# One batch for an expert product, a top-8 from the gate rows, and two groups of transposes moved from TensorE to DMA

## The chip, the cores and the metric

The kernel runs on one core of one Trainium2 chip. The metric is device time in microseconds (us) of one execution. The kernel before took 249.81 us (median of 3 runs, 249.35 to 250.25). A run also lists the span that the profile sees (some 1.8 us less than the time) and the mean clock granted to TensorE. A run is called slow when it is more than 1.5% above the fastest of its own kernel; ratios use fast runs only.

Names: PE is TensorE (matmuls), PEld its weight loads, DVE VectorE, ACT ScalarE, POOL GpSimd, SP SyncE, which only issues transfers here. Clock 1.00 is full speed.

## The reference

Two branches over the same 2048 rows of 1024 numbers, mixed by a gate. Branch A is a complex state-space scan; branch B adds an expert's output to eight chosen rows only.

```python
g = sigmoid((x * gate_w).sum(-1))                       # one gate per row
a = 2*Re(C @ scan(Lam_bar, B_bar @ x)) + x*Dskip        # the bulk of the work
idx = argsort(-(x @ w_r))[:8]                           # eight chosen rows
xs = x[idx]
y = (silu(xs @ w_gate) * (xs @ w_up)) @ w_down          # 1024 -> 3584 -> 1024
b = x;  b[idx] += y * sigmoid(r[idx])
out = g*a + (1-g)*b                                     # bf16, 1 x 2048 x 1024
```

Branch A keeps TensorE busy for almost the whole time. The expert must be squeezed between its matmuls.

## The kernel before

The program is a list of large blocks (`s1`: input product, `s2`: output product, each 16 matmuls of 128x512), and everything else is attached to positions in that list: `at((8, 1.9), f)` emits `f` in block 8 after its second piece. The parts that matter:

```python
def sel_c():                                   # eight chosen rows, transposed by PE
    for dc in range(KD):
        nc.tensor.transpose(xselT_ps[:, dc, :], xsel[:, dc*P:(dc+1)*P], ident[:NSEL, :NSEL])
    nc.scalar.copy(out=xselT[:, :, 0:NSEL], in_=xselT_ps[:])

def silu_t():                                  # the product silu(g)*u, transposed by PE
    for c in range(NFB):                       # NFB = 7
        nc.tensor.transpose(aT_ps[:, c]..., M["gr", 1][:, c*P:(c+1)*P], ident[:])
    nc.scalar.copy(out=M["aT"][:, :, :, 0:NSEL], in_=aT_ps[:, :, :, 0:NSEL])

# expert weights stream through slots of 1 MB (w_gate/w_up slots, then 7 of w_down);
# load_w() fills a slot from SP's queue as soon as its buffer is free
pos = [...] + [(8, 1.9)] * 4 + [(9, 2.9)] * 3  # y: first 64 matmuls, later 48

def skip_x(*bs):                               # rows scaled by (1-g): stored from ACT's queue
    nc.scalar.activation(out=xt[:], in_=xt[:], func=ACT.Copy, scale=omgcol[:, b:b+1])
    nc.scalar.dma_start(out2d[b*P:(b+1)*P, :], xt[:])
def fin(b):                                    # g*a added onto them: accumulating store, POOL
    nc.gpsimd.dma_start(out2d[b*P:(b+1)*P, :], ots.pop(b)[:], accum_op=ALU.add)
```

## Time and profile before

| before | value |
|---|---|
| span of the profiled execution | 248.3 us |
| PE busy | 242.7 us, 98% |
| DVE busy | 227.0 us, 91% |
| PE waits | 2.3 us in all, every one before 12 us |
| matmuls of y | 64 at 207.1 us, 48 at 226.3 us |
| last matmul of the last tile starts its run | 238.1 us |

The row to trust is PE's. The lines themselves, and what follows from them, stand in the prediction.

### The profile page before, as it was taken

To read this page: it belongs to the slowest core of one execution; us is meant where nothing else is said; L and a number is where in the kernel's file an instruction comes from. 1 tells how busy PE (TensorE), PEld (TensorE's weight loads), DVE (VectorE), ACT (ScalarE), POOL (GpSimd) and SP (SyncE) were. 2 spreads that over 40 slices of the span, in tenths; PEclk is the share of its full clock that TensorE was granted. 3 is DMA by queue.
4 is the path that set the end of the run, shared out by engine and by line. 5 is a ranking of instruction groups with operands and counts; after the bars stand their busy time and mean duration, and the time that the engine had idled before them with its cause. 6 is when DMAs were issued, how large, how long until landed. Compare 5 with 4: busy or idle time off the path is not lost.

```text
span 248.3 us, 3608 instructions
## 1 busy us (share of the span) xinstructions
PE 242.7 (98%) x1414; PEld 115.6 (47%) x1414; DVE 227.0 (91%) x231; ACT 117.4 (47%) x203; POOL 33.6 (14%) x50
## 2 busy tenths in 40 slices
PE   7899999999999999999999999999999999999995
PEld 5664444444444444444444444444444445445453
DVE  0899999999999999999999999999999999995954
ACT  3599973333345322282354571235267445537421
POOL 4000000000100003151402050100100211011810
PEclk9999999999999999999999999999999999999999
DMA  7999999999760000077976989877599972993053
GB/s 170 214 201 213 223 228 202 261 220 255 225 220 0 3 0 0 7 187 210 340 212 225 343 252 300 279 240 291 156 313 317 374 157 59 308 309 45 3 118 96
DMA packets 64193, 48.25 MB, mean 194 GB/s; under 512 B 49568, under 2 KB 51232, under 8 KB 64176
## 3 DMA queue, kind: packets, MB, share of 16 engines
q1 hardware_dynamic: 59120, 37.23, 55.5%
q0 software_dynamic: 3424, 7.90, 14.8%
q10 hardware_dynamic: 1632, 2.89, 3.8%
q8 instruction: 11, 0.18, 0.3%
q14 instruction: 6, 0.05, 0.1%
HBM read 27.55 MB, written 8.40 MB: 145 GB/s over the span
## 4 chain that ended last, share of the span: by engine, by line
PE 84%; DVE 7%; DMA 4%; SPq 3%; issue 0%; ACT 0%; DVEq 0%
PE zps L771 42%; PE vps L266 32%; DMA X<-in_A_x_dram 4%; PE zps L787 3%; PE pgu L660 3%; SPq L80 2%; PE vps L282 1%; PE y L672 1%; DVE U L302 1%; DVE U L313 1%; DVE H L340 1%; DVE U L338 1%; DVE H L336 1%; PE zr L487 1%; DVE S2tab L252 1%; DVE Ctab L251 1%
## 5 line engine op out<-in xcount | busy, mean ns | idle before, releaser
L771 PE MATMUL zps<-CT,H 128*128 128x512 bf16 x480 | 105.5, 379 | 0.0
L266 PE MATMUL vps<-X,BT 128*128 128x512 bf16 x480 | 105.1, 379 | 0.0
L266 PEld LDWEIGHTS <-BT 128*128 128x128 bf16 x480 | 46.4, 98 | 56.6 <-PE pgu L660 0.7
L771 PEld LDWEIGHTS <-H 128*128 128x128 bf16 x480 | 46.2, 98 | 56.3 <-issue 1.5
L313 DVE TENSOR_TENSOR_SCAN U<-d,U 128x2048 bf16<-128x2048 f32 (+2 forms) x22 | 62.0, 2860 | 1.0 <-DVE U L304 0.5
L273 ACT CAST V<-vps 128x512 bf16<-128x512 f32 x60 | 32.2, 588 | 56.3 <-PE vps L266 56.3
L776 ACT ACTIVATE ot<-zps,gcol 128x512 bf16<-128x512 f32 x30 | 20.6, 687 | 54.1 <-PE zps L771 54.1
L797 POOL DMA_DIRECT2D out_dram<-ot x14 | 13.0, 931 | 34.4 <-ACT ot L776 24.0
L303 DVE TENSOR_TENSOR V<-V,nTi 128x4096 bf16<-128x4096 bf16 (+2 forms) x11 | 16.7, 1517 | 0.5
L304 DVE TENSOR_TENSOR U<-U,V 128x4096 bf16<-128x4096 bf16 (+2 forms) x11 | 16.7, 1516 | 0.4
L302 DVE TENSOR_TENSOR U<-V,T2tab 128x4096 bf16<-128x4096 bf16 (+2 forms) x11 | 16.6, 1509 | 0.4
L338 DVE TENSOR_TENSOR U<-U,S2tab 128x4096 bf16<-128x4096 bf16 x7 | 16.0, 2292 | 0.2
L340 DVE TENSOR_TENSOR H<-H,U 128x4096 bf16<-128x4096 bf16 x7 | 16.0, 2292 | 0.2
L336 DVE TENSOR_TENSOR H<-U,Ctab 128x4096 bf16<-128x4096 bf16 x7 | 16.0, 2283 | 0.0
L745 ACT CAST zps<-xd 128x512 f32<-128x512 bf16 (+1 forms) x25 | 14.2, 575 | 3.2 <-ACT xt L732 2.9
L709 POOL DMA_DIRECT2D xt<-in_A_x_dram x12 | 7.1, 592 | 62.7 <-DMA out_dram<-xt 31.5
L732 ACT ACTIVATE xt<-xt,omgcol 128x1024 bf16<-128x1024 bf16 x12 | 13.8, 1146 | 0.0
L371 DVE TENSOR_TENSOR_SCAN U<-D,U 128x1024 bf16<-128x1024 f32 x4 | 8.9, 2271 | 0.1
L282 PE MATMUL vps<-X,BT 128*128 128x256 bf16 x64 | 7.5, 273 | 0.9 <-DMA X<-in_A_x_dram 0.6
L727 DVE TENSOR_TENSOR xd<-xt,Dbc 128x1024 bf16<-128x1024 bf16 x12 | 7.7, 682 | 0.3 <-ACT V L273 0.3
L282 PEld LDWEIGHTS <-BT 128*128 128x128 bf16 x64 | 6.1, 98 | 2.4 <-issue 0.7
L660 PE MATMUL pgu<-wgu,xsel 128*32 128x448 bf16 x128 | 7.2, 354 | 0.0
(161 smaller groups left out, 152.7 us busy)
## 6 DMA issues: line engine op xcount, KB each, us to landing
wgu<-in_B_w_gate_dram SPq DMA_DIRECT2D x16, 448.0 KB, 6.5
wgu<-in_B_w_up_dram SPq DMA_DIRECT2D x16, 448.0 KB, 5.8
wd<-in_B_w_down_dram SPq DMA_DIRECT2D x12, 512.0 KB, 7.6
out_dram<-ot POOLq DMA_DIRECT2D x14, 256.0 KB, 5.8
xt<-in_A_x_dram POOLq DMA_DIRECT2D x12, 256.0 KB, 4.2
out_dram<-xt ACTq DMA_DIRECT2D x10, 256.0 KB, 5.3
xt<-in_A_x_dram SPq DMA_DIRECT2D x4, 256.0 KB, 3.5
out_dram<-xt POOLq DMA_DIRECT2D x4, 256.0 KB, 3.4
```

The lines of the kernel that those rows point to most:

```text
L266: nc.tensor.matmul(o, lhsT=BT[pl][:, dc, ct * P:(ct + 1) * P], rhs=X[m][:, dc, k0 * LC:k1 * LC], start=(dc == 0), stop=(dc == KD - 1))
L273: nc.scalar.copy(out=V[k][:, :, ct, :], in_=vp[m, ct][:, :, kk, :])
L282: nc.tensor.matmul(vps[:, pl, c, :], lhsT=BT[pl][:, dc, ct * P:(ct + 1) * P], rhs=X[0][:, dc, k * LC:(k + 1) * LC], start=(dc == 0), stop= ...
L302: nc.vector.tensor_tensor(out=u, in0=v, in1=T2tab[:, :, c0:c1, :], op=ALU.mult)
L303: nc.vector.tensor_tensor(out=v, in0=v, in1=bc(nTi, c0, c1), op=ALU.mult)
L304: nc.vector.tensor_tensor(out=u, in0=u, in1=V[k][:, ::-1, c0:c1, :], op=ALU.add)
L313: nc.vector.tensor_tensor_scan(out=fl, data0=d0[:, c0:c1, :].rearrange("p c t -> p (c t)"), data1=fl, initial=0.0, op0=ALU.mult, op1=ALU.add)
L336: nc.vector.tensor_tensor(out=h, in0=g, in1=bc(Ctab, c0, c1), op=ALU.mult)
L338: nc.vector.tensor_tensor(out=g, in0=g, in1=S2tab[:, :, c0:c1, :], op=ALU.mult)
L340: nc.vector.tensor_tensor(out=h, in0=h, in1=G[k][:, ::-1, c0:c1, :], op=ALU.add)
L771: nc.tensor.matmul(zps[:], lhsT=H[k][:, pl, ct, tl * P:(tl + 1) * P], rhs=CT[pl][:, ct, dsl], start=(fresh and ct == 0 and pl == 0), stop= ...
L776: nc.scalar.activation(out=ots[b][:, dsl], in_=zps[:], func=ACT.Copy, scale=gcol[:, b:b + 1])
```

## The change

The intent is to take small work off PE. The gate vectors are transposed in a hole at the start; the top-8 search reads the gate rows as they lie; the chosen rows and the expert's product are transposed by DMA; y is computed in one batch. For that all seven `w_down` slots must be in SBUF together, so four of them go into the dead buffer of B (`BT`), and they are all loaded without a break.

```diff
+    vb_ps = ...; two nc.tensor.transpose(...)          # now ahead of s1x(1, 0)
 def sel_a():
-    nc.tensor.transpose(rT_ps[:], rcb[:], ident[:])
+    rT = rowp.tile([P, 2 * LC], F32); nc.scalar.copy(out=rT[:], in_=M["zrb"][:])
 def sel_b():
-    for k in range(2): nc.tensor.matmul(fl_ps[:, k, :], lhsT=ones16[:], ...)
+    nc.tensor.matmul(fl_ps..., lhsT=ones8[:], rhs=mm..., start=True, stop=True)
 def sel_c():
-    for dc in range(KD): nc.tensor.transpose(...)
-    nc.scalar.copy(out=xselT[:, :, 0:NSEL], in_=xselT_ps[:])
+    nc.sync.dma_start_transpose(xselT[:], xsel[:])
 def silu_t():
-    (seven nc.tensor.transpose, one nc.scalar.copy)
+    nc.sync.dma_start_transpose(M["aT"][:]..., M["gr", 1][:])
-    at((8, 0.8), silu_t)
+    at((7, 0.97), silu_t)
-    pos = ... [(8, 1.9)] * 4 + [(9, 2.9)] * 3
+    pos = ... [(8, 3.9)] * 7
+        if n == 7:                                      # B is dead: room for 4 slots
+            for pl in range(2):
+                t = const.tile([P, 4, 2, D], BF16, name="wdb", tag=f"BT{pl}")
+                free_w.extend(((t, 0), (t, 1)))
 ...                                                    # cuts: zs_ps moved to (8, 3.88), scatter earlier, skip_d(4) behind dve_m(5)
```

## The prediction

> **What bounds the kernel now.** I read the page's first part, then TensorE's waits, then the chain that ended last in order of time. The busy line of the page:
>
> ```profile
> PE 242.7 (98%) x1414; PEld 115.6 (47%) x1414; DVE 227.0 (91%) x231; ACT 117.4 (47%) x203; POOL 33.6 (14%) x50
> ```
>
> TensorE (PE) is busy for 242.7 of 248.3 us; VectorE (DVE) with 91% is second. All that PE waited for, from the view of PE's waits:
>
> ```profile
> PE wps L149 <- DVE halfpi L129: 1.1, 1, 1.1
> PE vps L282 <- DMA X<-in_A_x_dram: 0.6, 1, 0.6
> PE va_ps L161 <- DMA vrow<-in_A_Lambda_im_dram: 0.4, 1, 0.4
> PE vps L282 <- DMA BT<-in_A_B_im_dram: 0.2, 1, 0.2
> ```
>
> All four lie before 12 us. From 11.93 us to 245.24 us the chain is PE without a hole, apart from a detour over DVE at 36 to 61 us during which PE's own timeline is solid (208 matmuls of line 266 from 15.65 on). So a microsecond of PE work removed after 12 us is a microsecond of time, unless it opens a new wait. The pieces that the change touches, from the chain in order of time (start us, us, what):
>
> ```profile
> 15.58 0.13 PE vb_ps L440 x2
> ...
> 70.28 0.15 PE rT_ps L519
> ...
> 80.90 0.20 PE fl_ps L542 x2
> ...
> 101.93 0.28 PE xselT_ps L579 x8
> ...
> 109.23 0.27 PE zs_ps L595 x8
> ...
> 203.31 0.39 PE aT_ps L685 x7
> 203.70 3.45 PE zps L771 x16
> 207.16 1.86 PE y L672 x64
> 209.02 17.37 PE zps L771 x80
> 226.39 1.42 PE y L672 x48
> 227.81 10.47 PE zps L771 x48
> 238.28 6.96 PE zps L787 x48
> ```
>
> The whole side branch (selection of eight rows, their transposes, the expert product y) is small between blocks of 16 matmuls that take 3.45 us. Its removable part is about 1 us of 245: this caps the gain.
>
> The transfers matter for the second half of the change. The windows view (stretch, length, busy of PE, PEld, DVE, ACT, POOL, clock, DMA share, GB/s):
>
> ```profile
> 192.00:198.00 6.00, 6.00 (x30) 2.70 (x29) 5.86 (x7) 2.55 (x4) 1.47 (x2) 1.00 1.05 369
> 198.00:204.00 6.00, 6.00 (x35) 2.91 (x34) 5.93 (x7) 1.93 (x4) 0.89 (x1) 1.00 0.85 189
> 204.00:210.00 6.00, 6.00 (x84) 3.37 (x83) 5.90 (x4) 4.02 (x7) 0.86 (x1) 1.00 0.22 38
> 210.00:216.00 6.00, 6.00 (x29) 2.74 (x28) 5.72 (x6) 2.31 (x3) 0.00 (x0) 1.00 1.00 297
> ```
>
> The DMA engines are full up to about 200 us (the first four down-projection slots, 4 x 1 MB), nearly idle up to 210, and full again (the last three slots, whose buffers only come free when the first part of y is computed).
>
> **What the Trainium skill says.** "VectorE: DVE Perf Modes", section The three transpose paths, gives a 128x128 bf16 transpose as 390 ns on TensorE and 1309 ns on the DMA crossbar. The trace disagrees on what TensorE saves: seven such transposes take 0.39 us of PE's path together, 56 ns each, since they are pipelined. "DMA: Bandwidth & Descriptors", section DMA Transpose (X-bar), restricts it to 2-byte types, a partition count that is a multiple of 16, and the SP or ACT queue; this explains why the eight chosen rows are now padded to 32 and why both new transposes stand in SP's queue. All 21 transposes of the kernel before are in SP's queue too, so the trace agrees as far as it goes. The same page, Queues, rings and completion order, says that each queue has one ring on each DMA engine and that the engines take turns between queues. I take from it that the product's transpose, issued behind seven megabytes of weights on the same queue, moves after them. No run shows this yet.
>
> **The change part by part.**
> 1. Two transposes for the gate vectors (0.13 us at 15.58) go ahead of the second small matmul group. PE waits there 0.57 us for X (up to 11.93), and the vectors landed at 6.9 and 7.0 us. They fit into that hole: -0.13.
> 2. Top-8 now reads the gate pass rows directly, four rows of 512 on 128 partitions instead of 16 of 128. The transpose rT_ps goes: -0.15. One matmul of 64 columns replaces two of 128 (0.20): at about 0.07, as each of the two in piece 1, -0.12 or so. DVE: the 16x128 maximum took 0.275 us, and a DVE pass here costs some 1.04 ns per element (1225 ns for 1024 f32, 174 ns for 16), so the 512-long maximum and index search cost +0.4 each, +0.8; the two mm passes, ci, the second maximum and search, the two eq passes and the last sum are 96 elements shorter each, eight times 0.1 back. Net about 0 on DVE.
> 3. The chosen rows go through DMA: eight PE transposes, -0.28, and one ACT copy less. The gather landed at 100.3 us, the DMA engines are idle, and the rows are first needed at the first expert matmuls at 113 us. A 256 KB transpose of B landed 4 to 5 us after its issue; 64 KB here should be in by 106. Hidden, with 7 us to spare, and SP's queue has nothing else to do until 113.
> 4. The gate of the chosen rows (zs_ps, 0.27) only moves, to just before y: 0.
> 5. The product through DMA: seven PE transposes, -0.39, and an ACT copy.
> 6. One batch: y costs (1.86 - 1.42)/16 = 0.0275 us per matmul and 0.10 per batch, so 112 in one cost 3.18 instead of 3.28: -0.10.
>
> Sum on PE's path: 0.13 + 0.15 + 0.12 + 0.28 + 0.39 + 0.10 = 1.17 us. 249.81 - 1.17 = 248.64 if nothing new waits.
>
> What may wait is y itself. Four slots of weights now go into the space of B, free after the last input product (184.9 us), so all seven load without a break. PE ends the block before y at 215.93 in the kernel before; minus the transposes (0.39), the first y part (1.86) and what was saved or moved earlier (0.13 + 0.15 + 0.12 + 0.28 + 0.27 = 0.95) is 212.7, plus zs_ps 0.27: y wants to start at 213.0. Its inputs: the eighth 512 KB piece landed at about 200.3 in the kernel before (the seventh at 199.05, at 1.35 us apiece), 199.4 on the new clock. Six more follow, at 1.35 us each as between 194 and 200, or at 1.9 as between 212.4 and 222 when stores run beside them: 207.5 to 211. Behind them comes the transpose of the product (224 KB), another 2 to 3 us: 209.5 to 214, an estimate, the middle near 211.8. So there is some 1 us of slack in the middle and a wait of 1 us at the bad end. I put 0.4 us on it on average.
>
> The end of DVE's work improves, but off the path. The row that shows it:
>
> ```profile
> 229.56 0.53 DVE L696 TENSOR_SCALAR yc<-yc,rsel_c,omg 8x1024 bf16<-8x1024 bf16 x1 [2.57 <-ACT yc L691]
> ```
>
> DVE sat 2.57 us waiting for y before its last scan, and the last half of H was only ready 1.0 us before PE took it (237.26 against 238.28). With y at 213 to 216 that wait goes, the last scan starts near 227.6 instead of 230.0, and the margin grows to some 3 us. PE never waited there, so this earns nothing, but it means that PE's saving isn't eaten by DVE.
>
> Predicted: 249.81 - 1.17 + 0.4 = 249.0.
>
> **The rivals.**
> - The wait for y's inputs is long: if the SP queue is slower (316 GB/s in the second burst, with the accumulating stores of the output beside it) and the transpose from SBUF is costly, aT lands at 215 to 217, PE stands 2 to 4 us, and the time is 250.6 to 252.6. For it: DMA share 1.0 in both bursts, and a queue in order. Against: 7 us of idle DMA between the bursts, half of what three slots need.
> - DVE becomes the bound: it is at 91% and PE gets faster by 1 us. Against: PE has no wait on DVE after 2 us, the output blocks take H some 5 us or more after it is written (52.7 against 66.8, 75.9 against 80.9, 209.3 against 215.9), and the tight spot at the end loosens. It would make the time about 249.8.
> - The shorter tail pays: the scatter of the eight rows, its read-back and the last stores come earlier, and more than 1.2 us is won. Against: the last instructions before the end wait for PE's last matmuls at 245.24, and then for a store of 1.6 us; the read-back was in by 241.3. It would make 247.5 at the most.
> - The scatter now lies before two output stores on GpSimd instead of one, and takes 7.15 us to land. If these stores ended last, the time would grow by a microsecond. Against: DVE frees the scatter some 3 us earlier, so the stores end by 243, as the last of them did before.
>
> **Range and chances.** The gain is bounded by 1.2 us, with 0.1 for the terms I estimated. The loss is bounded by the wait for y: about a third that it shows at all, a tenth that it is over 2 us. Three runs of before spread over 0.9 us. Hence 248.2 to 250.8. Two per cent is 5 us: faster by that 1%, slower 3%, within 96%.
>
> **What would show it.** PE's count of matmuls falls by 17, to 1397, and its busy time by about 1. In the chain rT_ps, xselT_ps and aT_ps are gone, vb_ps stands before 12 us, fl_ps is one matmul, y is one piece of 112 with about 3.2 us. PE's waits: as before with the X wait down to 0.4; if a wait of line 670 on a DMA (the product's transpose or a weight slot) appears, its length is the stall that I gave 0.4 on average. DVE's wait for yc is gone. DMA: no idle stretch between 201 and 209 us, one after 213. The prediction is wrong if that stall is over 2 us, if PE waits for DVE or ACT somewhere new, or if the time falls by more than 1.7 us.

## The result

The changed kernel took 256.81 us (median of 4 runs, 256.08 to 259.81) against 249.68 us for the kernel before on the same chip. A ratio here is the mean time of one kernel's fast runs over that of the other's in the same rounds, so it is not quite the ratio of the medians: 1.0255, with a 95% interval of 1.0203 to 1.0308. (A fifth run of the changed kernel, 254.74 us, is outside the median and counts in the ratio.) It is slower by 2.5%, outside the predicted range of 248.2 to 250.8.

The first profile fell in an execution of 259.8 us (span 258.0), one of the longer ones. A second one, taken later in a fast execution (`e9_after_again`, span 255.4), shows the same picture a little smaller. The page of the first: busy times, then the granted clock in 40 slices (9 is 90% or more).

```profile
PE 242.3 (94%) x1373; PEld 116.5 (45%) x1397; DVE 227.2 (88%) x231; ACT 117.4 (45%) x200; POOL 33.5 (13%) x50
...
PEclk9999999999999999999999999999999997599999
```

PE's weight loads fell by 17, to 1397, as the change wants, but its share is now 94%, and there is a dip of the clock near 85% of the span. PE's waits (engine, line, what for: total, times, longest):

```profile
PE y L670 <- DMA aT<-gr: 7.9, 1, 7.9
PE wps L149 <- DVE halfpi L129: 1.1, 1, 1.1
PE vps L282 <- DMA BT<-in_A_B_re_dram: 0.8, 1, 0.8
PE pgu L658 <- DMA wgu<-in_B_w_up_dram: 0.7, 2, 0.5
```

One wait dwarfs the others: the first matmul of y waits 7.9 us for `aT`, the product transposed by DMA. PE's own timeline (start us, length, what):

```profile
212.64 0.34 PE L587 MATMUL zs_ps<-rg,xsel 128*8 128x1 bf16 x8
220.86 1.90 PE L670 MATMUL y<-wd,aT 128*32 128x256 bf16 x32 [7.88 <-DMA aT<-gr]
...
225.96 0.90 PE L670 MATMUL y<-wd,aT 128*32 128x256 bf16 x16
```

PE was ready for y at 213.0, where the prediction had it. It stood until 220.9, and then y took 5.9 us (226.79, the next block, minus 220.86) in place of 3.2. The windows view says why (columns as in the prediction: the clock is the number before the last two):

```profile
210.00:216.00 6.00, 2.93 (x20) 1.28 (x19) 5.79 (x5) 2.54 (x5) 0.85 (x1) 1.00 1.23 98
212.00:214.00 2.00, 0.98 (x12) 0.34 (x10) 1.97 (x2) 0.95 (x4) 0.27 (x1) 1.00 0.57 76
214.00:216.00 2.00, 0.00 (x0) 0.00 (x0) 1.86 (x3) 0.00 (x0) 0.58 (x1) 1.00 0.28 31
216.00:222.00 6.00, 1.14 (x24) 0.86 (x28) 5.83 (x6) 0.00 (x0) 0.00 (x0) 0.53 0.99 160
222.00:228.00 6.00, 5.95 (x101) 3.96 (x95) 5.90 (x7) 1.01 (x3) 0.00 (x0) 0.62 0.01 3
```

While PE stood, its clock fell to half (0.53 is the mean of 216 to 222; the trace has it at 0.50 from 216.3), and it came back only with y's last matmul, at 226.5. The sum closes: 7.9 of wait, 2.7 of slow clock in y (5.9 - 3.2), 0.5 more in the small waits (2.8 against 2.3), minus the 1.17 saved, is 9.9 us; the spans differ by 9.7.

The transposing transfer itself (name view of `aT`: issue time on SP's sequencer, then issue to landing):

```profile
L681 SPq DMA_TRANSPOSE aT<-gr x1: 10523/10523/10523, 199.9 to 199.9; - x1
...
DMA to landing us min/median/max: 20.9/20.9/20.9
```

SP needed 10.5 us only to issue it, and it landed 20.9 us after 199.9, at 220.8. In front of it in the queue stood the seven slots of `w_down`, in 14 pieces of 512 KB. The thirteenth landed at 212.3. The last one left no landing in the trace; its packets (2048 bytes on that queue, from the trace's packet records) moved until 215.3; the 213.6 in the expectation of e2 below stands in no view.

The transpose's packets (256 bytes) began at 209.5, before the weights were through; 374 of the 896 had started by 213 and the last did so at 219.7. The two windows from 212 to 216 above show that this was no lack of bandwidth: with weights, transpose and stores all unfinished, the DMA engines were busy for 0.57 and 0.28 of the time. The dip is in the second profile too (0.28 from 212 to 214). Its cause is not known.

One more line of the changed kernel belongs here. DVE waits in the middle of the kernel for a load of rows (timeline of DVE):

```profile
129.55 0.69 DVE L722 TENSOR_TENSOR xd<-xt,Dbc 128x1024 bf16<-128x1024 bf16 x1 [4.48 <-DMA xt<-in_A_x_dram]
```

In the kernel before the same load landed at 125.3 and DVE did not wait. Here it landed at 129.5. In this profile PE never waits for DVE after the start, so the stall costs nothing here; it matters below.

### The profile page after: what moved, and what is told of

The parts are those of the page before. It is cut to its first block, busy times and chain, and to the rows that moved or that the text cites.

```text
span 258.0 us, 3549 instructions
## 1 busy us (share of the span) xinstructions
PE 242.3 (94%) x1373; PEld 116.5 (45%) x1397; DVE 227.2 (88%) x231; ACT 117.4 (45%) x200; POOL 33.5 (13%) x50
## 4 chain that ended last, share of the span: by engine, by line
PE 76%; DMA 18%; SPq 3%; issue 1%; DVE 0%
PE vps L266 37%; PE zps L766 30%; DMA wgu<-in_B_w_up_dram 8%; DMA aT<-gr 8%; PE zps L782 3%; PE y L670 2%; DMA X<-in_A_x_dram 2%; SPq L80 2%; PE pgu L658 2%; PE vps L282 1%; SPq L629 1%; PE zr L486 1%; SPq L77 0%; DVE ot L787 0%; PE zt L493 0%
## 5 line engine op out<-in xcount | busy, mean ns | idle before, releaser
L766 PE MATMUL zps<-CT,H 128*128 128x512 bf16 x469 | 104.2, 379 | 0.5
L266 PEld LDWEIGHTS <-BT 128*128 128x128 bf16 x480 | 46.7, 98 | 56.8 <-PE pgu L658 0.7
L670 PE MATMUL y<-wd,aT 128*32 128x256 bf16 x48 | 2.8, 401 | 7.9 <-DMA aT<-gr 7.9
L796 DVE TENSOR_TENSOR ot<-ot,xt 128x512 bf16<-128x512 bf16 x3 | 1.3, 426 | 9.1 <-ACT ot L784 4.8
```

The lines of the kernel that those rows point to most:

```text
L266: nc.tensor.matmul(o, lhsT=BT[pl][:, dc, ct * P:(ct + 1) * P], rhs=X[m][:, dc, k0 * LC:k1 * LC], start=(dc == 0), stop=(dc == KD - 1))
L766: nc.tensor.matmul(zps[:], lhsT=H[k][:, pl, ct, tl * P:(tl + 1) * P], rhs=CT[pl][:, ct, dsl], start=(fresh and ct == 0 and pl == 0), stop= ...
```

## The experiments

Theory at the start: PE stands at y because the product's transpose lands late, and loses its clock by standing. Why the transpose is late had three candidates: its SBUF source or the transpose itself, its place behind seven slots in a queue, and other transfers beside it. All kernels gave correct results. The first four ran with the kernel before at 249.96 us (39 runs), the next four at 249.71 (23 runs).

**e1_quiet**: the kernel before, plus four transposes of the same size while the DMA engines are idle.

```diff
+    for _ in range(2):
+        nc.sync.dma_start_transpose(aT, H[1]...[:, 0:FG])      # from SBUF
+        nc.sync.dma_start_transpose(aT, x2d[0:P, 0:FG])        # from HBM
+    at((2, 0.5), quiet)
```

> The kernel before, with four extra transposes of 128x896 bf16 into the product's tile between 76 and 96 us, where its DMA engines are idle: from SBUF, from HBM, from SBUF, from HBM, each waiting for the one before. Theory QUEUE (the product's transpose was late because it stood behind seven megabytes in the same queue) and theory MIX (it is slow only while other traffic runs beside it): issue 1.2 to 4.2 us and landing within 6 us of the issue, from either source. Theory SOURCE (a transpose that reads SBUF is slow by itself): from SBUF some 10.5 us of issue and 15 to 21 us to landing, from HBM 1.3 and 5. The time stays at that of before within 1% in all cases, except under SOURCE, where the gather and the expert weights at 113 us could be held up by some us.

One run, 251.32 us (only one look). The name view of `aT`:

```profile
L844 SPq DMA_TRANSPOSE aT<-H x2: 1222/1238/1254, 76.4 to 82.3; - x2
L845 SPq DMA_TRANSPOSE aT<-in_A_x_dram x2: 1222/1222/1222, 79.4 to 85.2; - x2
...
DMA to landing us min/median/max: 2.9/2.9/2.9
```

Issue 1.2 us, landing after 2.9 us, from SBUF as from HBM. The prediction's "another 2 to 3 us" was right for a quiet transpose. Neither the source nor the transpose as such makes it late.

**e2_product_pe**: the changed kernel with the product transposed by PE again.

```diff
-        nc.sync.dma_start_transpose(M["aT"][:]..., M["gr", 1][:])
+        (seven nc.tensor.transpose and one copy, as before)
-    at((7, 0.97), silu_t)
+    at((8, 0.8), silu_t)
```

> The changed kernel with only the product's transpose put back on TensorE (seven transposes, after the first output product of the second last block but one). All theories that blame the DMA transpose: no wait of y on aT, y batch 3.2 us at full clock, at most 1 us of wait for the last weight slot (landed about 213.6 in the changed kernel, y starts at about 213): 249.0 us, between 248.4 and 250. If instead the seven slots in one burst are the trouble, y waits for a weight slot by several us and the time stays above 252.

250.07 us (248.63 to 251.89, 20 runs), ratio 0.9996 (0.9977 to 1.0016). The wait at y is gone, y starts at 213.3 and takes 3.2 us. So against the kernel before, the loss hangs on this one transfer. In the profile PE's last run of matmuls starts at 237.24, against 238.12 in the kernel before: 0.88 us earlier. The medians do not show that gain.

**e3_product_dma**: the kernel before with only the product's transpose on DMA. It then stands behind four slots of weights, not seven.

```diff
-        (seven nc.tensor.transpose and one copy)
+        nc.sync.dma_start_transpose(M["aT"][:]..., M["gr", 1][:])
-    at((8, 0.8), silu_t)
+    at((7, 0.97), silu_t)
```

> The kernel before with only the product's transpose moved to DMA, at the place that the changed kernel gives it: behind four weight slots instead of seven, y still in two batches. QUEUE: it is issued at 196 us, the four slots end at 200.3, it lands by 204, y at 207 doesn't wait, 249.2 us. SOURCE: issue until 206, landing near 216, y waits about 9 us, with the lost clock 260 us. MIX: two accumulating stores and two loads run between 195 and 205, so it lands between 205 and 213: 250 to 257 us.

250.12 us (249.34 to 250.65, 12 runs), ratio 1.0002 (0.9982 to 1.0021).

```profile
L682 SPq DMA_TRANSPOSE aT<-gr x1: 1419/1419/1419, 196.7 to 196.7; - x1
...
DMA to landing us min/median/max: 6.8/6.8/6.8
```

Behind four slots the issue is 1.4 us and the landing at 203.4, before y wants it at 206.7. Transposing the product by DMA is harmless in itself.

**e4_transpose_first**: the changed kernel, but the last three weight slots are requested after the transpose.

```diff
-        if n == 7: (all four BT slots at once)
+    def fill_b(): (three BT slots); load_w()
+    at((7, 0.98), fill_b)                              # just after silu_t
```

> The changed kernel with the order in SP's queue changed: the product's transpose goes before the last three weight slots (which go into B's space only then) instead of behind them. QUEUE: it lands by 204, the three slots follow from 201 on and land by 213: 248.8 us, at most 250. SOURCE: SP issues it for 10.5 us, so the three slots start after 208 and land after 218; y waits 6 us or more: above 255. MIX: between the two.

250.42 us (249.15 to 253.18, 12 runs), ratio 1.0024 (0.9988 to 1.0061). The issue took 1.3 us at 197.1 and the data were in by about 202. Now y waits for what stands last instead:

```profile
PE y L670 <- DMA wdb<-in_B_w_down_dram: 0.9, 1, 0.9
```

So the order in the queue is the lever: the same bytes, another order, and six microseconds less (though not the 250 at most that I had expected).

**e5_no_company**: the changed kernel with the stores of tiles 9 to 13 asked for later.

```diff
+    at((9, 0.11), lambda: (fin(9), fin(10), fin(11), skip_x(12), skip_x(13)))
-    (their five places in blocks 7 and 8)
```

> The changed kernel, the product's transpose behind seven weight slots as there, but the three accumulating stores and the two scaled-row stores that ran beside it between 200 and 220 us are issued only after y. Theory MIX (the transpose is slowed by stores of other queues in flight): it lands within 3 us of the last weight slot, near 214, y waits at most 2 us, 248.5 to 251 us. Theory DEPTH (the transpose's descriptors, issued into a queue that is full, are what makes it late): issue still about 10 us, landing 217 or later, y waits 4 us or more, 253 to 257 us.

252.71 us (252.17 to 254.01, 4 runs), ratio 1.0131 (1.0091 to 1.0171). Only half of the edit took effect: the accumulating stores still went out at 207.5 and 214.4 (206.8 and 213.7 in the changed kernel), and only ACT's two stores moved. The transpose landed at 215.2, the wait at y was 1.5 us, the clock stayed at 1.00. The time lies between the two theories. Moving the scaling had a price of its own, a wait of 1.0 us of PE for ACT.

**e6_drained**: the transpose held back until the last weight slot has landed.

```diff
 def silu_t():
+    nc.gpsimd.tensor_scalar(out=z[:], in0=w_last[0:1, 1, 0, 0:1], scalar1=0.0, ...)
+    nc.gpsimd.tensor_tensor(out=gr1[0:1, 0:1], in0=gr1[0:1, 0:1], in1=z[:], op=ALU.add)
```

> The changed kernel, all stores as there, but the product's transpose is issued only when the last weight slot has landed (a tiny GpSimd pair of operations reads that slot and touches the product). DEPTH: the queue is empty then, issue 1.3 us, landing 3 to 5 us after it: issue at about 212, landing 215 to 217, y waits 2 to 4 us: 250.5 to 253.5 us, better than the changed kernel although it starts 12 us later. MIX: the same stores are in flight, so landing stays at 219 or later: 254 to 258 us.

261.25 us (256.03 to 262.00, 4 runs, three of them slow; no ratio). The weights landed later than I had assumed (GpSimd's instruction that waits for the last slot started at 215.6), so the issue came at 217.1 instead of 212. It took 1.3 us, and y began at 221.7, after a wait of 7.5 us and again with a lost clock (y took 5.9 us). From issue to use are 4.7 us although an accumulating store ran beside it: with the queue empty the transpose is quick again, but an empty queue comes too late.

**e7_company**: the kernel before plus two transposes at 105 us, beside GpSimd's transfers and no weights.

```diff
-    at((2, 3.5), lambda: (rows(1), fin(0), fin(1)))
+    at((2, 3.5), lambda: (rows_mul(), beside(), rows_ld(), fin(0), fin(1)))
```

> The kernel before with two extra transposes of 128x896 (one from SBUF, then one from HBM) at 105 us, when SP's queue is empty but GpSimd's queue runs two stores, two loads and two accumulating stores. MIX: either takes 6 us or more to land, at least twice the 2.9 us of the quiet place, and the stores beside it land later too. DEPTH: issue 1.3 us, landing within 4.5 us.

One look, 249.65 us. The first landed within 3.7 us of its issue, beside plain stores and loads; the second, issued when the first had landed, took 7.9 us beside two accumulating stores (against 2.9 quiet). But loads and plain stores ran beside it too.

**e8_act_queue**: the changed kernel with the product's transpose on ACT's queue, where nothing stands in front of it.

```diff
-        nc.sync.dma_start_transpose(M["aT"]...)
+        nc.scalar.dma_start_transpose(M["aT"]...)
-    at((7, 0.97), silu_t)
+    at((7, 3.96), silu_t)
```

> The changed kernel with the product's transpose issued from ACT's queue, which is empty, instead of SP's, at about 200 us, while the weights still stream in SP's queue and the stores run as there. DEPTH: issue 1.3 us, landing 203 to 208, y waits for the last weight slot at most (0 to 2 us): 248.5 to 251 us. MIX: landing after 212, y waits 2 us or more: over 252 us.

250.73 us (248.66 to 253.29, 20 runs), ratio 1.0035 (1.0014 to 1.0055).

```profile
L681 ACTq DMA_TRANSPOSE aT<-gr x1: 1312/1312/1312, 200.1 to 200.1; - x1
...
DMA to landing us min/median/max: 14.4/14.4/14.4
```

The issue is 1.3 us; the 7 to 10 us of the other versions go with the place behind seven slots. But the data still landed only at 214.5, when the weights in the other queue were nearly through (their last piece at 215.5). So neither theory has it whole (the time fits the first, the landing the second), and two things were wrong with the picture of a tidy row: an own queue does not let the transpose overtake the weights by much, and a long issue is not what makes it late.

The next four share the kernel before at 249.56 us (43 runs, two of them slow at 258.15 and 285.82 us and left out of the ratios).

**e9_after_again**: the changed kernel, unedited.

> The changed kernel itself, unedited, to see a fast execution in the profile (its first profile fell in the slow state). My theory: the product's transpose lands last, because it stands behind seven slots of weights and runs beside the two stores of scaled rows, and the wait is so long that the granted clock drops for the batch y. Then fast runs lie at 255.5 to 257.5, the wait of line 670 on the transpose is 4.5 to 7 us, the transpose lands at 217.5 to 220, and y takes 4 to 6 us instead of 3.2. Rival: the wait in the first profile was a thing of the slow state; then it is below 3 us here and y takes 3.2 us, and the loss of some 7 us lies elsewhere.

255.34 us (253.81 to 257.19, 4 runs), ratio 1.0214 (1.0162 to 1.0266). In a fast execution:

```profile
219.12 1.90 PE L670 MATMUL y<-wd,aT 128*32 128x256 bf16 x32 [6.44 <-DMA aT<-gr]
...
223.62 0.60 PE L670 MATMUL y<-wd,aT 128*32 128x256 bf16 x16
```

The wait is 6.4 us and y takes 5.0 us. It is no artefact of the first profile. The last 16 matmuls, in 0.60 us, are at full speed again; the clock came back at 223.0, 3.9 us after PE resumed.

**e10_stores_behind**: the changed kernel with the two stores of scaled rows on SP's queue, behind the transpose.

```diff
-                nc.scalar.dma_start(out2d[b * P:(b + 1) * P, :], xt[:])
+                q = nc.sync if b in (12, 13) else nc.scalar
+                q.dma_start(out2d[b * P:(b + 1) * P, :], xt[:])
```

> The changed kernel, with the two stores of scaled rows (tiles 12 and 13) issued on the sync queue, behind the product's transpose, in place of the scalar queue beside it; all computation stays where it was, so the scalar-engine side effect of the earlier run without company is gone. My theory, that these two stores beside the transpose cost some 5 us and that the rest of its lateness is its place behind the weights: landing at 214 to 216, a wait of 1.0 to 2.5 us at y, full clock, y 3.1 to 3.3 us, and 250.3 to 251.8 (ratio 1.003 to 1.009). Rival, that the accumulating stores alone jam it: landing still at 218 to 221, a wait of 5 us or more, a dropped clock in y, and 254.5 or more.

254.71 us (252.69 to 256.29, 4 runs), ratio 1.0230 (1.0186 to 1.0275). The profiled execution was the best of the four; the transpose landed at 214.7 in it, as my theory wanted. The times say otherwise: the ratio is that of the unedited kernel. Had I read only the profile, I would have called this theory confirmed. The profile still shows something about the clock:

```profile
214.75 1.52 PE L670 MATMUL y<-wd,aT 128*32 128x256 bf16 x32 [2.05 <-DMA aT<-gr]
...
219.04 0.61 PE L670 MATMUL y<-wd,aT 128*32 128x256 bf16 x16
```

A wait of 2.05 us was already enough to lose the clock (it stood at 0.50 from 215.2 to 218.6, so it fell only after PE had resumed, and y took 4.8 us); after 1.55 us in e5 and 1.65 in e8 it was kept (3.2 us).

**e11_old_weights**: the kernel before with everything of the change except the one batch of y and the new place of the weights.

```diff
 (before) + gate transposes early, top-8 from gate rows, chosen rows and product by DMA
```

> The kernel before with all of the change except the one batch of y and the new place of the weights: gate transposes early, top-8 from the gate rows, chosen rows by DMA, product by DMA behind only four slots, y in two batches as before. If each removed piece of TensorE work is worth its time: 0.13 + 0.15 + 0.12 + 0.28 + 0.39 = 1.07 us less, so about 248.7, ratio 0.996. Rival: TensorE then runs ahead of the weights of the gate and up projections and of the first inputs and waits for them (0.5 us or more at line 658), so at most half is left: ratio 0.998 to 1.000. No wait at y in either.

249.17 us (248.22 to 251.44, 22 runs), ratio 0.9992 (0.9975 to 1.0010): the rival's figure. No wait at y; 0.4 us at the weights of the up projection, and a wait of 2.0 us of DVE for the load of tile 7.

**e12_y_later**: the changed kernel, y in one batch but three output blocks later. No transfer is touched.

```diff
-    pos = ... [(8, 3.9)] * 7        +    pos = ... [(9, 2.9)] * 7
-    at((8, 3.92), fin_a)            +    at((9, 2.92), fin_a)
     (what reads y follows at (9, 2.95))
```

> The changed kernel with the one batch y, unchanged in itself, placed three output blocks later (after 223 us instead of 213), and what follows from y with it; every transfer stays as in the changed kernel. My theory, that the loss is only TensorE standing at y and the clock it loses there: no wait of line 670 (the transpose lands at 215 to 221, before 223), y takes 3.2 us, clock 1.0, and 248.6 to 249.5 (ratio 0.995 to 0.999, since 0.5 us of the 1.17 may go to waits for weights of the first projections). Rival, that the transfers or the reordered work of the change cost time elsewhere too: 250.5 or more with no wait at y.

250.45 us (248.41 to 254.03, 22 runs), ratio 1.0030 (1.0008 to 1.0053).

```profile
222.78 1.06 PE L670 MATMUL y<-wd,aT 128*32 128x256 bf16 x32
```

The transpose is as clumsy as ever (issue 7.9 us, landing at 216.1), but y no longer wants it before 222.8: no wait, full clock, 3.2 us, and a span of 246.8. Most of the loss is back, so most of it lay at y. But the median is above the expected 248.6 to 249.5 and at the edge of the rival's 250.5, and the runs spread over far more than most of those of the kernel before: the rival is right in part, and something else was left.

Two causes were open: why the transpose's landing differs from one execution to the next, and what spreads e12. The next four share the kernel before at 249.02 us (13 runs).

**e13_adds_after**: one tiny GpSimd instruction that reads `aT`, meant to hold back the accumulating stores from tile 10 on.

```diff
+        nc.gpsimd.tensor_scalar(out=z[:], in0=M["aT"][0:1, 0, 0, 0:1], scalar1=0.0, ...)
-    at((8, 2.5), lambda: fin(10))
+    at((8, 2.5), lambda: (gate(), fin(10)))
```

> The changed kernel with one tiny GpSimd instruction that reads one element of the transposed product, put before the accumulating store of output tile 10: from there on the accumulating stores can't start before the transpose has landed. The stores of scaled rows stay beside it. Theory A, that the accumulating stores beside the transpose make it late: landing by 213.5 to 215, a wait at y of at most 2 us in all executions, clock 1.0, 249.3 to 251.5 (ratio 0.999 to 1.007). Rival B, that the company doesn't matter and the place behind seven slots on one queue does it all, with a size that differs from execution to execution: no change, 253.5 to 257 (ratio 1.018 to 1.027).

254.90 us (253.07 to 255.58, 4 runs), ratio 1.0217 (1.0182 to 1.0252): the figure of rival B, landing at 216.4, wait 4.9 us. But the edit did less than it says. The scheduler put the instruction behind the store of tile 10, which still went out at 205.4, and only tile 11's was held back.

**e14_alone**: the same, with the two stores of scaled rows behind the transpose too.

```diff
 (e13) + q = nc.sync if b in (12, 13) else nc.scalar      # as in e10
```

> The same with the two stores of scaled rows also behind the transpose on the sync queue, so that from 206 us on nothing else moves beside the weights and the transpose. Theory A: as in the run before it or better, 249.0 to 251 (ratio 0.997 to 1.006), landing by 213 to 214.5. Rival C, both kinds of stores matter together: only this one recovers (ratio below 1.007) while the run before it stays above 1.012. Rival B: 253 or more here too, and then what makes the transpose late is the weights in front of it in the queue alone.

254.97, 254.22, 254.34 and 249.58 us. By the 1.5% rule the first three are slow and there is no ratio, but the mean clocks (0.984 to 0.985 in the three, 1.000 in the fourth) suggest that the wait at y was there in three executions and hardly in the fourth. Only one was profiled. In the profile (a long one) the landing was at 216.1 and the wait 4.6 us.

**e15_later_again**: e12 once more, for a second profile.

> Once more the kernel with the one batch y three output blocks later, for a second profile: its runs spread from 248.4 to 254.0, its one profiled execution had no wait at all. If this execution is one of the long ones (over 250), theory A expects that the transpose lands after 223 us in it and y waits by as much as the time is over 248.6; the rival expects no wait at y, and the loss in another place (first inputs or weights of the first projections).

One run, 250.15 us: a longer one, as hoped. It has no wait at y, as the rival expected; the transpose landed at 218.4. PE's waits, and DVE's:

```profile
PE pgu L658 <- DMA wgu<-in_B_w_up_dram: 0.8, 1, 0.8
PE zps L782 <- DVE H L385: 0.8, 1, 0.8
```

```profile
DVE xd L722 <- DMA xt<-in_A_x_dram: 3.9, 1, 3.9
```

PE now waits for DVE, in the last tile, for H. And DVE is late because it stood 3.9 us for the load of tile 7 at 125 us, 100 us earlier: at 91% busy it does not catch up. In e12's profile, the 246.8 us one, that stall was 1.7 us and PE did not wait. So the second rival of the prediction, DVE as the bound, can come true once PE's own wait is gone; e17 tests it.

**e16_later_alone**: y later, with e14's edits.

```diff
 (e12) + gate() before fin(10), as in e13
       + q = nc.sync if b in (12, 13) else nc.scalar
```

> The batch y three output blocks later and nothing beside the transpose. If the spread of the later version came from a transpose that sometimes lands after 223 us, it is gone here: 248.3 to 249.3 with a spread like the kernel before (ratio 0.995 to 0.999). If it stays at 250 to 252 in half of the runs, the excess isn't y's wait, and lies in a part of the kernel that all versions with the new place of the weights or the reordered side branch share.

250.84 us (249.89 to 253.11, 8 runs), ratio 1.0078 (1.0050 to 1.0106). Again no wait at y. DVE stood 4.6 us for the load, and PE waited for it in two places:

```profile
PE zps L767 <- DVE H L340: 1.1, 2, 0.9
...
PE zps L783 <- DVE H L385: 1.0, 1, 1.0
```

The last two kernels share the kernel before at 249.26 us (29 runs).

**e17_later_no_dve_stall**: e12 with two of DVE's jobs swapped.

```diff
-    at((3, 6.5), lambda: (skip_d(3), dve_post(3, 0, 8)))
+    at((3, 6.5), lambda: (dve_post(3, 0, 8), skip_d(3)))
```

> The version with the one batch y three output blocks later, and one line of VectorE's order swapped: the product with the skip weights for tiles 6 and 7 (which waits for the load of tile 7 at 125 us, 0.4 to 4.6 us in the versions so far) comes after the three passes for H of that block instead of before them. Theory: what was left of the loss in the later version is this stall, which makes the last H late by a microsecond. Then VectorE's wait for that load is gone, no wait of the last output blocks on H, and 248.3 to 249.0 with a spread below 2 us (ratio 0.993 to 0.998 against before). Rival: the spread of 248.4 to 252 stays; ratio 1.002 or more; then the loss comes from another wait, such as that for the weights of the up projection.

248.54 us (247.53 to 252.04, 22 runs), ratio 0.9973 (0.9955 to 0.9991), span 246.6. This is the first version that beats both kernels, by 0.3% against the one before. All that PE waits for in its profile:

```profile
PE wps L149 <- DVE halfpi L129: 1.1, 1, 1.1
PE pgu L658 <- DMA wgu<-in_B_w_up_dram: 0.6, 1, 0.6
PE vps L282 <- ACT rdec L183: 0.3, 1, 0.3
```

DVE's stall for the load is gone and so is every wait on H. The spread is not quite: 17 of 22 runs lie between 247.5 and 248.9, five between 249.8 and 252.0, so the hoped-for 2 us was exceeded.

**e18_truly_alone**: e14 with the gate one store earlier.

```diff
-    at((7, 3.95), lambda: fin(9))       +    at((7, 3.95), lambda: (gate(), fin(9)))
-    at((8, 2.5), lambda: (gate(), fin(10)))   +    at((8, 2.5), lambda: fin(10))
```

> The changed kernel with y in its place, the stores of scaled rows behind the transpose, and the accumulating store of tile 9 too held back until the transpose has landed (in the last three such runs that one store, issued at 205 us, still ran beside it, and landed within 1.1 us of it every time). Theory, that this accumulating store and the transpose hold each other up: landing by 210 to 213.5, a wait of 0 to 1.5 us, full clock, 248.7 to 250.3 in all executions (ratio 0.999 to 1.005). Rival, that seven slots of weights in front of it are enough: landing still at 214.5 to 217 and 252 to 255 in most executions (ratio 1.012 or more).

250.29, 251.02, 252.44, 254.75, 255.93 and 256.28 us; the first three count as fast, ratio 1.0074 (1.0036 to 1.0111). The scheduler again put the gate after the store at 206.6 (tile 10's, not tile 9's as my text has it), so this was e14 a second time and not the test it was meant to be. Landing 217.2, wait 4.4 us.

**The landings together** (profiled executions; all have seven slots in front of the transpose or beside it):

| version | beside it from 205 us on | landing, us | wait at y | y took |
|---|---|---|---|---|
| changed kernel, e9 | 2 ACT stores, 2 accumulating | 220.8, 219.1 | 7.9, 6.4 | 5.9, 5.0 |
| e12, e15, e17 | the same | 216.1, 218.4, 217.9 | none | 3.2 |
| e13 | 2 ACT stores, 1 accumulating | 216.4 | 4.9 | 5.8 |
| e5, e10 | 2 accumulating | 215.2, 214.7 | 1.5, 2.1 | 3.2, 4.8 |
| e14, e18, e16 | 1 accumulating | 216.1, 217.2, 216.9 | 4.6, 4.4, none | 5.8, 6.0, 3.2 |
| e8 (own queue) | 2 ACT stores, 2 accumulating | 214.5 | 1.6 | 3.2 |

Nothing with seven slots landed before 214.5, while y, where it kept its place, wants its input at 211.6 to 213.7. Of the versions that use SP's queue, the six with both ACT stores beside it landed at 218.1 in the mean, the five without at 216.0. So these stores cost some 2 us at most in the profiles, and the times of e10, no better than those of the unedited kernel, do not bear even that out. The place behind seven slots is what all of them share.

## Why the prediction was wrong

**The step that failed** is in the timetable of y's inputs: "Behind them comes the transpose of the product (224 KB), another 2 to 3 us: 209.5 to 214, an estimate, the middle near 211.8", and the 0.4 us put on it. It failed in two terms.

- The weights: I had the last of them at 207.5 to 211. The eighth piece landed at 199.9, near my 199.4, but the thirteenth only at 212.3: about 2.5 us a piece, where I had 1.35 to 1.9. Packets of the last moved until 215.3; in e6 it was in by 215.6.
- The transpose: it landed at 220.8, 5.5 us after those last packets and 8.5 us after the thirteenth piece, where I had 2 to 3 us behind the weights. The 2.9 us of a quiet transpose (e1), or the 6.8 behind four slots (e3), do not carry over to one behind seven slots. e4 shows that the order is the lever, since the same transfers with the transpose in front brought 1.0024. My reading that it "moves after" the weights held only for its landing: its packets began at 209.5, and in a queue of its own (e8) it landed hardly before the earliest of the others (214.5 against 214.7).

**The term that was missing** is the clock. The first rival, a long wait for y's inputs, is what happened; I gave it a loss of 1 to 3 us because I counted the wait alone. Where the wait was 2 us or more, y took another 1.7 to 2.8 us longer than its 3.2, at a clock of 0.50 that came back 3.9 to 5.8 us after PE resumed. The Trainium skill has the mechanism ("TensorE: Matmul & The Clock Gate", section Why this matters for your kernels: no idle gaps of PE above about 3 us, or the clock falls back); I had not looked it up, since no wait was in the kernel before. The traces agree in kind: 1.65 us kept the clock, 4.4 to 7.9 us lost it; but 2.05 us lost it too (e10), less than the page's figure. The rival's arguments were off as well: 316 GB/s stands in no view that I asked for (297 and 353 in the windows from 210 and 216), and 7 us of idle DMA is more than half of what three slots need, 8.1 to 11.4 us at my own 1.35 to 1.9 us a piece.

**Point by point, what held.**
- Pieces 1, 2, 3 and 5: the removed work is gone from PE's sequence, loads fell by 17 to 1397. The gate transposes lie at 11.3 us in the hole, the one `fl_ps` matmul took 0.12 to 0.19 us. On DVE the 512-long maximum and its search took 0.69 us each (predicted 0.275 + 0.4).
- The chosen rows by DMA: issued at 99.8, issue 1.2 us, packets through by 101.8. Hidden, as predicted (though the transposes of B that it was compared with took 4.0 to 5.8 us, not 4 to 5).
- y wants to start at 213.0: it did. That it fits to the tenth is luck: PE had by then waited 0.5 us more than in the kernel before, and other executions were ready between 211.6 and 213.7. One batch of y takes 3.18 us at full clock: 3.2 in e2, e5, e8, e12 and e17.
- DVE's wait for yc fell from 2.57 to 0.2 us, and earned nothing, as predicted. The margin beside it was misread: 237.26 is the end of a first pass over the second half of H. The half that PE takes first was ready at 236.65, 1.5 us before PE's last run at 238.12. In e15 it was ready at 237.31, and PE waited 0.8 us for it.
- The sum of 1.17 us: it is in the profiles (0.88 in e2; a span of 246.6 in e17 against 248.3) and partly in the times (0.72 us between e17's median and that of the kernel before). In e11, with 1.07 of it, the medians differ by 0.4 us and the interval includes no gain.

**What I had not seen** is where the rest of the gain goes. PE ahead of time by 1 us meets waits that were hidden: 0.4 to 1.6 us for weights of the up projection in several versions, and the last H. The second rival, DVE as the bound, was argued away with margins from the kernel before, in which DVE had not waited for the load of tile 7. In the profiles of the versions with the change's early part and no swap, that stall was between 1.0 and 5.5 us. e15 and e16 show its end in PE's waits, and e17, with two jobs swapped, takes it away.

**What stays open.** Why the landing varies from 214.5 to 220.8 us, and from execution to execution, is not settled, nor why the engines stand mostly idle before it: the dip of the first profile is in e12 too (a share of 0.32 from 211 to 213), and not in e8 (1.09 and 1.08 from 210 to 214), where the transpose landed earliest. One accumulating store, issued at about 206, was beside the transpose in every version with seven slots in front of it, and landed within 1.0 us of it in all twelve profiles of the table; both attempts to hold it back failed at the scheduler. Whether they hold each other up is suggested by e7 and not shown. Nor is it known why the load of tile 7 takes 3.3 us in the kernel before and 7.2 in e16.

## What to carry to other kernels

A transfer that a busy engine will wait for belongs in front of the bulk transfers of its queue, or its reader belongs later; work out its landing from a transfer under the same load, not from a quiet one. When a wait of TensorE is possible at all, price it with the clock that it may lose, which here was 1.7 to 2.8 us on top of the wait. And when an edit gains in the profile of one execution, look at the times of all: those of one version lay up to 6 us apart here (e18).

## What the Trainium skill lacked or had wrong

- "DMA: Bandwidth & Descriptors", section Rules for kernel authors, says that a transpose next to ordinary DMAs needs nothing. That holds for correctness. For time it does not: 2.9 us quiet, 7.9 us beside accumulating stores (e7), 14.4 to 20.9 us with seven slots of weights in front of it or beside it.
- "Advanced Engine Details and Errata", section X-Bar Transpose (TRN2), says that transposing DMAs are as fast as regular ones. A 224 KB transpose took 2.9 us alone, in line with it (so did a plain load of 256 KB at 106.9 us in the kernel before); behind 7 MB of weights it landed 20.9 us after its issue, 5.5 us after the last of their packets (220.8 against 215.3).
- No page that I read gives the time a queue's engine needs to issue a transfer into a full queue: 1.2 to 1.4 us for a transpose with at most four slots ahead or an empty queue, 7.1 to 10.5 us behind seven.
- "TensorE: Matmul & The Clock Gate", section Why this matters for your kernels, puts the gap that costs the clock at about 3 us. Here 1.65 us kept it, and 2.05 us (after 0.34 us of one-column matmuls) already lost it in one execution, where the clock stood at 0.50 for 3.4 us. In the first profile it did so for 10.2 us, and 128x256 matmuls took up to 421 ns in place of 273.
- "VectorE: DVE Perf Modes", section The three transpose paths, compares single transposes (390 ns on TensorE). Seven in a row cost PE 56 ns each in the kernel before, so moving them off PE is worth less than that page suggests: 0.39 us for all seven.
